# Tying the second MLP's weight decodings to their written place, and grouping its products into longer runs of matmuls

## The chip, the cores and the metric

One core of one Trainium2 chip runs the whole program. The engines that matter here are TensorE (PE; its weight loads stand apart as PEld), VectorE (DVE), ScalarE (ACT) and SyncE (SP), which here issues the DMA transfers. The metric is the device time of one execution in microseconds, the median of several runs.

## The reference

Everything is float32: 4 batches of 8 heads of 576 positions with 64 columns go through a linear attention, and the 2304 tokens of 512 columns that come out go through two MLPs with 2048 hidden columns.

```python
kv = einsum('bhsd,bhse->bhde', k, v)
out = einsum('bhsd,bhde->bhse', q, kv)
x = out / sqrt(mean(out * out, -1) + 1e-06) * g_norm      # as 2304 x 512
h = x @ w_in1;  x = (h * tanh(softplus(h))) @ w_out1      # first MLP
h = x @ w_in2                                             # second MLP
return (maximum(h, 0) + alpha * minimum(h, 0)) @ w_out2
```

## The kernel before

Every operand of a matmul is held as a high and a low part, and each product is three matmuls (`three`, L127 to L129): high by high, high by low, low by high. The weights come from DRAM as pairs of 32-bit words and are decoded on the chip: a scaling on ScalarE (`w_scale`, L387), three bit operations on VectorE (`w_bits`, L393, L394, L397), a cast to the high part on ScalarE (`w_high`, L432) and a subtraction for the low part on VectorE (`w_low`, L436). Each such operation covers 128 x 512 values.

**The first MLP** runs in 80 slots (NS = 80): five blocks of tokens by 16 blocks of hidden columns. In slot s TensorE does 12 matmuls of the first layer (tile `h`), ScalarE the activation of slot s-1 (`mish`, L502), ScalarE and VectorE split the result of slot s-2 into high and low (`g_split`, L495 and L496: tiles `gh`, `gl`), and TensorE does 12 matmuls of the second layer for slot s-4 (tile `acc`). The attention for later blocks is done between them.

**The second MLP** computes in three passes over 768 tokens, each of 8 units of hidden columns; the text numbers these units 0 to 23. A unit forms seven products of sums of blocks (`product`, "1", "6", "2", "7", "5", "4", "3"; six matmuls of 128 x 384 each, tile `pp`) and combines them to four blocks of the hidden layer, "11", "22", "21" and "12". The products share two banks of PSUM: 1, 2, 7 and 4 use one in turn, 6, 5 and 3 the other, so a product can start only when the sum that reads the last one in its bank has run (for product 2 the copy L805 on ScalarE, for 4 and 3 the sums L816 and L820 on VectorE, through the tiles `tx` and `ty`). Each block gets its PReLU (`prelu1`, L756 and L759), a cast to high on ScalarE (L761) and a subtraction for the low part on VectorE (L762, tiles `g` and `xb`), and enters the output by a chunk of nine matmuls of 128 x 512 (`chunk`, tile `acc`). A unit takes four quarters, one call of `unit` each: product 1, then the chunk of block 22 of the unit before; products 6 and 2, chunk 21 of the unit before; products 7 and 5, chunk 12 of the unit before; products 4 and 3, chunk 11 of the unit itself.

The second MLP's weights are prepared during the first MLP and the first pass. First-layer weights are decoded in eight pairs by `prep_unit` (five steps, with sums at L616 to L622 and splits at L572 and L573), written to DRAM (`put_unit`, L581, tile `wd`) and read back (`fetch`, `load_s`). Second-layer weights, 16 blocks j, are loaded by `load_out` (L375, tile `ws`) and decoded by `prep_out`. The table UNITS says in which slot or quarter (counted on from 80) a pair starts; t0 in the planning loop does it for the 16 blocks. The tokens' sums for the products are made from `xr` tiles, read from DRAM by L692 and added at L679, with high parts at L685 and low parts at L686.

TensorE's order is the written one from slot 20 on. On VectorE, ScalarE and SyncE a scheduler orders the instructions by its own timing, so an operation may stand well ahead of the place where it is written; each engine then runs its list strictly in order. Waiting for a transfer is part of an instruction, and whatever stands behind it on that engine waits too.

Of the kernel before, what the change touches and what calls it, by code (L numbers as in the profile page):

```python
# [13 lines left out]
ALU = mybir.AluOpType  # L14
# [19 lines left out]
EARLY = 4  # L34
WHEN = {1: (8, 3, 1, 2, 3, 6), 2: (4, 4, 1, 2, 3, 6), 3: (0, 5, 1, 2, 4, 5), 4: (0, 5, 1, 2, 4, 5)}
MANUAL = 20
IN_X = (4, 6)
UNITS = (36, 46, 51, 62, 65, 68, 70, 85)
BY32 = 2
FIRST = "p0 c0 p1 c1 p2 p3 c2 c3 w4 u0 w5 u1".split()  # L40
# [9 lines left out]
def attn_moe_moe2(  # L50
# [30 lines left out]
    nc = tc.nc  # L81
# [6 lines left out]
    NJ = DFF // P  # L88
# [4 lines left out]
    NS = NB * NJ  # L93
    NU = NJ // 2
    QW = 2 * P
    NPASS = NT // (2 * HT)
# [101 lines left out]
    def bank(tag, nm):  # L198
        if tag == "at":
            turn[0] += 1  # L200
            tag = f"at{turn[0] % 2}"
        pool = ps_h if tag == "h" else ps_a if tag[:2] == "at" else ps_acc
        return pool.tile([P, 512], F32, tag=tag, name=nm)
# [158 lines left out]
    def stage(nm, dt, cols):  # L362
        return st.tile([P, 2 * DM], dt, tag="ws", name=nm, bufs=3)[:, :cols]
# [164 lines left out]
    room1, xt, raw, pr, gg, tmp, acc1 = {}, {}, {}, {}, {}, {}, {}  # L528
# [56 lines left out]
    def place(i, nm):  # L585

        if (i, nm) not in places:
            if i not in IN_X:
                t = stage(nm, I32, 2 * DM) if nm in ("r0", "r1", "x") else st.tile([P, DM], F32, tag="wf", name="wf")
# [63 lines left out]
    def load_s(u, k):  # L653
        if u < NPASS * NU:
            room1["load"] = nc.sync.dma_start(out=f32(room1["ring"][k]), in_=wd["s", u % NU, k])
# [76 lines left out]
    def first_of(u, k):  # L732

        i = u % NU
        if k in "753":
            s = room1["ring"]["753".index(k)]
            h, l = s[:, :QW], s[:, QW:]
        else:
            h, l = w1[1, 2 * i + (k in "64")]
            h, l = ((t[:, QW:] if k in "24" else t[:, :QW]) for t in (h, l))  # L740
        return [(h[:, a * P : (a + 1) * P], l[:, a * P : (a + 1) * P]) for a in range(2)]

    def product(u, k):
        more = {"2": "1", "4": "7", "3": "5"}.get(k)
        if more:
            pr[u, k] = pr.pop((u, more))
        else:
            pr[u, k] = bank("h", "pp")[:, :HT]
        h, l = xt[TERMS[k]]
        for a, w in enumerate(first_of(u, k)):  # L750
            three(pr[u, k], w, (h[a], l[a]), not more and a == 0, a == 1, skip_group_check=bool(more))

    def prelu1(u, nm, src, out):
        j = 2 * (u % NU) + (nm[0] == "2")
        t = tmp["u"]
        nc.vector.tensor_scalar(  # L756
            out=t, in0=src, scalar1=0.0, scalar2=acol[:, j : j + 1], op0=ALU.min, op1=ALU.mult
        )
        nc.vector.scalar_tensor_tensor(out=out, in0=src, scalar=0.0, in1=t, op0=ALU.max, op1=ALU.add)  # L759
        h, l = gg[nm]  # L760
        nc.scalar.copy(out=h, in_=out)  # L761
        nc.vector.tensor_tensor(out=l, in0=out, in1=f32(h), op=ALU.subtract)  # L762

    def next_r():
        tmp["r"].reverse()
        return tmp["r"][0]
# [32 lines left out]
    def unit(u, step, before):  # L799

        x = tmp["x"]
        tt = nc.vector.tensor_tensor
        if step == 0:
            product(u, "1")
            nc.scalar.copy(out=x, in_=pr[u, "1"])  # L805
            before()
        elif step == 1:
            product(u, "6")
            tt(out=x, in0=pr.pop((u, "6")), in1=x, op=ALU.add)
            product(u, "2")  # L810
            prelu1(u, "11", pr.pop((u, "2")), next_r())
            before()
        elif step == 2:
            product(u, "7")
            r = next_r()
            tt(out=r, in0=pr[u, "7"], in1=x, op=ALU.add)  # L816
            load_s(u + 1, 0)
            product(u, "5")
            load_s(u + 1, 1)
            tt(out=r, in0=pr[u, "5"], in1=r, op=ALU.add)  # L820
            prelu1(u, "22", r, r)
            before()
        else:
            product(u, "4")
            r = next_r()
            tt(out=r, in0=pr.pop((u, "4")), in1=x, op=ALU.add)
            prelu1(u, "21", r, r)
            product(u, "3")
            load_s(u + 1, 2)
            tt(out=x, in0=pr.pop((u, "3")), in1=x, op=ALU.add)  # L830
            prelu1(u, "12", x, x)
            before()

    early, after, late, hook, mid, fin, last = ({} for _ in range(7))

    def add(d, s, f, *a):
        d.setdefault(s, []).append((f, a))

    def run(d, s):
        for f, a in d.pop(s, []):  # L840
            f(*a)

    new_kv = {1: 1, 2: 2, 3: 3}
    for i in range(1, NB):
        h0, step, dk, do, dm, db = WHEN[i]
        h0 += (i - 1) * 2 * NJ
        for p in range(NP):
            h = h0 + p * step
            pre, before = early, max((h - step + dk) // 2 + 1 if p else h // 2 - 2, EARLY)
            if i == 1 and p == 2:  # L850
                pre, before = after, before - 1
# [21 lines left out]
    for j in range(NJ):  # L873
        if j >= EARLY and (1, j) not in early_w:
            add(late, max(j - 3, EARLY), load_w, 0, 1, j)
            add(mid, j - 2, w_begin, 0, 1, j)
        if (2, j) not in early_w:
            add(early, max(j + 1, EARLY), load_w, 0, 2, j)
            add(last, j + 2, w_begin, 0, 2, j)
            add(mid, j + 3, w_end)  # L880
        add(early, max(NS - NJ + max(j, EARLY) + 1, UNITS[j // 2] + 6), fetch, 1, j)
        t0 = NS - 10 + 3 * j // 2 if j < 8 else NS + 2 * (j - 7)
        add(early, t0, load_out, j)
        add(fin, t0 + 2, prep_out, j, t0 + 2 < NS)
    for i, s in enumerate(UNITS):
        add(late, s, load_unit, i, 0)
        add(late, s + 1, load_unit, i, 1)
        for step in range(5):
            add(fin, s + (1, 2, 2, 3, 4)[step], prep_unit, i, step)
        for step in range(3):  # L890
            add(late, s + 3 + step, put_unit, i, step)
    add(early, NS - 5, rooms1)
    for n in range(2):
        add(early, NS - 5 + 2 * n, first_raw, n)
# [5 lines left out]
    for n in range(1, NPASS):  # L900
        t0 = NS + 4 * NU * n
# [4 lines left out]
    def front(s):  # L906
        if EARLY <= s <= NS:
            mish(s - 1)
# [19 lines left out]

    LATER = ("22", "21", "12", "11")

    def quarter(n):

        s = NS + n
        u, step = divmod(n, 4)
        run(early, s)
        run(late, s)

        def before():
            front(s)
            run(mid, s)  # L940
            back(s)
            if step == 3 or u:
                chunk(u if step == 3 else u - 1, LATER[step])

        if u < NPASS * NU:
            unit(u, step, before)
        else:
            before()
        run(fin, s)
        run(last, s)  # L950

# [31 lines left out]
    with tc.manual_schedule():  # L983
# [14 lines left out]
        for h in range(2):  # L998
            r = slice(h * D, (h + 1) * D)
# [5 lines left out]
        for p in range(NP):  # L1005
            for h in range(2):
                r = 32 * p + 16 * h
# [3 lines left out]
                    out=rows, in0=f32(rows), in1=ident[:, r + 1 : r + 2].to_broadcast([P, D]), op=ALU.add  # L1011
# [46 lines left out]
```

## Time and profile before

| what | value |
|---|---|
| median of 3 runs | 867.41 us (865.24 to 868.76) |
| the profiled execution's own time | 868.87 us |
| its span | 866.9 us |
| TensorE busy | 837.7 us (97%) |
| VectorE busy | 554.3 us (64%) |
| ScalarE busy | 317.6 us (37%) |

The profiled execution stands 1.5 us above the median. A row of a timeline gives an instruction's start and duration; matmuls overlap, so their spacing is read from one start to the next. What stands in brackets is the time that the engine was idle before it and what released it.

### The profile page before, as it was taken

What the parts mean: (1) busy time and instruction counts of PE and PEld (TensorE: products, weight loads), DVE (VectorE), ACT (ScalarE), POOL (GpSimd) and SP (SyncE); (2) the same over time, 40 slices, a digit from 0 to 9 for tenths busy, and PEclk for the clock granted to TensorE, in tenths of its full rate; (3) what the DMA queues carried; (4) which work ended last, traced back from release to release, by engine and by line L of the source; (5) the groups of instructions that cost most, each with busy time, mean ns of one, the idle gap of its engine ahead of it and who ended that gap; (6) DMA issues with size and microseconds to landing.
All of it is one profiled execution on the core that took longest, in us unless ns stands there. A gap on an engine that the chain in (4) does not pass through costs nothing.

```text
span 866.9 us, 11632 instructions
## 1 busy us (share of the span) xinstructions
PE 837.7 (97%) x4408; PEld 712.6 (82%) x4408; DVE 554.3 (64%) x1062; ACT 317.6 (37%) x619; POOL 1.3 (0%) x7
## 2 busy tenths in 40 slices
PE   7999899989999999999999989999999999999997
PEld 5678677888878887887888878898889888989996
DVE  5888966272576145655795797569665568655654
ACT  3776445434443254334564332114211124211111
POOL 0000000000000000000000000000000000000000
PEclk9999899999999999999999999999999999999999
DMA  9756464514631033027984741141321141411211
GB/s 242 223 153 190 143 159 98 123 24 92 222 134 25 1 132 135 1 97 277 349 333 158 244 156 50 37 134 49 110 63 47 52 132 37 134 49 37 61 49 73
DMA packets 84743, 104.58 MB, mean 121 GB/s; under 512 B 34768, under 2 KB 58832, under 8 KB 84688
## 3 DMA queue, kind: packets, MB, share of 16 engines
q1 hardware_dynamic: 84688, 103.84, 39.1%
q8 instruction: 35, 0.57, 0.3%
q14 instruction: 20, 0.16, 0.1%
HBM read 79.70 MB, written 24.12 MB: 120 GB/s over the span
## 4 chain that ended last, share of the span: by engine, by line
PE 73%; DVE 11%; DMA 9%; ACT 3%; SPq 2%; issue 2%; DVEq 0%; ACTq 0%
PE acc L127 12%; PE acc L129 12%; PE acc L128 12%; PE h L127 6%; PE pp L127 6%; PE pp L129 6%; PE pp L128 6%; PE h L128 6%; PE h L129 6%; DMA r<-in_moe_w_in_dram 2%; DMA v<-in_v_dram 2%; SPq L180 2%; DVE wf L394 1%; PE kvps L211 1%; DVE wf L397 1%
## 5 line engine op out<-in xcount | busy, mean ns | idle before, releaser
L127 PE MATMUL acc<-gh,w 128*128 128x512 f32 (+1 forms) x320 | 119.9, 375 | 0.9 <-ACT n L502 0.4
L129 PE MATMUL acc<-gh,w 128*128 128x512 f32 (+1 forms) x320 | 118.2, 369 | 0.0
L128 PE MATMUL acc<-gl,w 128*128 128x512 f32 (+1 forms) x320 | 118.2, 369 | 0.0
L127 PE MATMUL h<-x,w 128*128 128x512 f32 (+1 forms) x240 | 91.6, 381 | 4.6 <-ACT n L502 4.5
L129 PE MATMUL h<-x,w 128*128 128x512 f32 (+1 forms) x240 | 89.7, 374 | 0.8 <-DVE w L436 0.7
L128 PE MATMUL h<-x,w 128*128 128x512 f32 (+1 forms) x240 | 89.2, 372 | 0.0
L496 DVE TENSOR_TENSOR gl<-n,gh 128x512 fp32r<-128x512 f32 (+1 forms) x80 | 50.8, 634 | 57.2 <-ACT gh L495 56.8
L129 PE MATMUL acc<-w,g 128*128 128x512 f32 x216 | 85.6, 396 | 0.2
L761 ACT CAST g<-ty 128x384 fp32r<-128x384 f32 x48 | 24.8, 516 | 140.0 <-DVE ty L759 135.9
L495 ACT CAST gh<-n 128x512 fp32r<-128x512 f32 (+1 forms) x80 | 46.3, 579 | 66.1 <-PE acc L129 65.7
L127 PEld LDWEIGHTS acc<-gh,w 128*128 128x128 f32 x320 | 60.6, 189 | 12.0 <-ACT n L502 0.9
L129 PEld LDWEIGHTS acc<-gh,w 128*128 128x128 f32 x320 | 60.4, 189 | 10.6 <-DVE w L436 0.4
L128 PEld LDWEIGHTS acc<-gl,w 128*128 128x128 f32 x320 | 60.5, 189 | 9.7
L127 PEld LDWEIGHTS h<-x,w 128*128 128x128 f32 x240 | 45.6, 190 | 17.3 <-ACT n L502 7.0
L502 ACT ACTIVATE n<-h 128x512 f32<-128x512 f32 (+1 forms) x80 | 44.5, 556 | 34.7 <-DVE gl L496 33.8
L128 PE MATMUL acc<-w,xb 128*128 128x512 f32 x144 | 56.8, 395 | 0.0
L128 PE MATMUL acc<-w,g 128*128 128x512 f32 x144 | 56.8, 395 | 0.0
L127 PE MATMUL acc<-w,g 128*128 128x512 f32 x144 | 56.0, 389 | 0.0
L127 PE MATMUL acc<-w,xb 128*128 128x512 f32 x144 | 56.0, 389 | 0.0
L129 PEld LDWEIGHTS h<-x,w 128*128 128x128 f32 x240 | 45.7, 190 | 9.4 <-DVE w L436 1.6
L128 PEld LDWEIGHTS h<-x,w 128*128 128x128 f32 x240 | 45.7, 190 | 7.3
L129 PEld LDWEIGHTS acc<-w,g 128*128 128x128 f32 x216 | 40.5, 187 | 9.6 <-DVE g L762 1.1
(202 smaller groups left out, 1684.1 us busy)
## 6 DMA issues: line engine op xcount, KB each, us to landing
xb<-wd SPq DMA_DIRECT2D x72, 256.0 KB, 2.7
ws<-in_moe_w_out_dram SPq DMA_DIRECT2D x32, 512.0 KB, 4.3
ws<-in_moe_w_in_dram SPq DMA_DIRECT2D x16, 512.0 KB, 4.4
r<-in_moe_w_in_dram SPq DMA_DIRECT2D x12, 512.0 KB, 5.1
wd<-r SPq DMA_DIRECT2D x12, 512.0 KB, 3.5
w<-wd SPq DMA_DIRECT2D x12, 512.0 KB, 5.7
k<-in_k_dram SPq DMA_DIRECT2D x16, 288.0 KB, 3.8
v<-in_v_dram SPq DMA_DIRECT2D x16, 288.0 KB, 4.2
```

The source lines that it names most:

```text
L127: nc.tensor.matmul(ps, lh, rh, start=start, stop=False, **kw)
L128: nc.tensor.matmul(ps, lh, rl, start=False, stop=False, **kw)
L129: nc.tensor.matmul(ps, ll, rh, start=False, stop=stop, **kw)
L180: nc.sync.dma_start(out=t[r : r + 32, C * p0 : C * (p0 + n)].rearrange("p (b d) -> p b d", d=32), in_=q[b, h, s : s + C * n, d : d + 32].r ...
L211: nc.tensor.matmul(ps[hs, hs], kt[:, h, j, :], vt[:, h, j, :], start=(j == 0), stop=(j == KVJ - 1))
L394: nc.vector.scalar_tensor_tensor(out=si, in0=high, scalar=-0x80000000, in1=si, op0=ALU.bitwise_and, op1=ALU.bitwise_or)
L397: nc.vector.scalar_tensor_tensor(out=si, in0=high, scalar=3, in1=si, op0=ALU.logical_shift_left, op1=ALU.bitwise_or)
L495: nc.scalar.copy(out=gh, in_=g)
L496: nc.vector.tensor_tensor(out=gl, in0=g, in1=f32(gh), op=ALU.subtract)
L502: nc.scalar.activation(out=g, in_=hps.pop(kk)[:, :T], func=AF.Mish)
L761: nc.scalar.copy(out=h, in_=out)
```

## The change

Three things change. First, `behind` wraps each `prep_unit` and `prep_out`: their instructions are ordered after the VectorE and ScalarE instructions that are written just before them, so they cannot stand earlier in these engines' lists. Second, the places are written anew: second-layer blocks 0 to 5 are decoded in slots 72 to 79 and loaded two slots earlier; blocks 6 to 15 are decoded in quarters 0, 1, 4, 5, 16, 17, 20, 21, 24 and 25 of the second MLP and loaded four quarters earlier; the last pair of first-layer weights (place 85) has its steps spread over quarters 8 to 16 with later puts and a later fetch. Third, twelve units (9 to 14 and 17 to 22) are done by `long_unit`: products 1, 6, 2 together, then two chunks of the unit before, then products 7, 5, 4, 3 together, then chunk 12 of the unit before and chunk 11 of the unit itself.

```diff
--- before.py
+++ after.py
@@ -35,6 +35,8 @@
 WHEN = {1: (8, 3, 1, 2, 3, 6), 2: (4, 4, 1, 2, 3, 6), 3: (0, 5, 1, 2, 4, 5), 4: (0, 5, 1, 2, 4, 5)}
 MANUAL = 20
 IN_X = (4, 6)
+SOON = 6
+OUTS = (0, 1, 4, 5, 16, 17, 20, 21, 24, 25)
 UNITS = (36, 46, 51, 62, 65, 68, 70, 85)
 BY32 = 2
 FIRST = "p0 c0 p1 c1 p2 p3 c2 c3 w4 u0 w5 u1".split()
@@ -830,6 +832,42 @@
             tt(out=x, in0=pr.pop((u, "3")), in1=x, op=ALU.add)
             prelu1(u, "12", x, x)
             before()
+
+    def long_unit(u, step):
+
+        x = tmp["x"]
+        tt = nc.vector.tensor_tensor
+        if step == 0:
+            product(u, "1")
+            nc.scalar.copy(out=x, in_=pr[u, "1"])
+            product(u, "6")
+            tt(out=x, in0=pr.pop((u, "6")), in1=x, op=ALU.add)
+            product(u, "2")
+            prelu1(u, "11", pr.pop((u, "2")), next_r())
+        elif step == 2:
+            product(u, "7")
+            r = next_r()
+            tt(out=r, in0=pr[u, "7"], in1=x, op=ALU.add)
+            load_s(u + 1, 0)
+            product(u, "5")
+            load_s(u + 1, 1)
+            tt(out=r, in0=pr[u, "5"], in1=r, op=ALU.add)
+            product(u, "4")
+            r2 = next_r()
+            tt(out=r2, in0=pr.pop((u, "4")), in1=x, op=ALU.add)
+            product(u, "3")
+            load_s(u + 1, 2)
+            tt(out=x, in0=pr.pop((u, "3")), in1=x, op=ALU.add)
+            prelu1(u, "22", r, r)
+            prelu1(u, "21", r2, r2)
+
+    def behind(f, *a):
+
+        with ExitStack() as stack:
+            for e in (mybir.EngineType.DVE, mybir.EngineType.Activation):
+                prev = next(i for i in reversed(nc.cur_bb.bb.instructions) if i.engine == e)
+                stack.enter_context(tc.issue_after(prev))
+            f(*a)
 
     early, after, late, hook, mid, fin, last = ({} for _ in range(7))
 
@@ -878,17 +916,18 @@
             add(early, max(j + 1, EARLY), load_w, 0, 2, j)
             add(last, j + 2, w_begin, 0, 2, j)
             add(mid, j + 3, w_end)
-        add(early, max(NS - NJ + max(j, EARLY) + 1, UNITS[j // 2] + 6), fetch, 1, j)
-        t0 = NS - 10 + 3 * j // 2 if j < 8 else NS + 2 * (j - 7)
-        add(early, t0, load_out, j)
-        add(fin, t0 + 2, prep_out, j, t0 + 2 < NS)
+        add(early, max(NS - NJ + max(j, EARLY) + 1, UNITS[j // 2] + (6 if j // 2 < NU - 1 else 14)), fetch, 1, j)
+        t0 = NS - 8 + 3 * j // 2 if j < SOON else NS + OUTS[j - SOON]
+        add(early, t0 - (2 if j < SOON else 4), load_out, j)
+        add(fin, t0, behind, prep_out, j, j < SOON)
     for i, s in enumerate(UNITS):
+        steps, puts = ((1, 2, 2, 3, 4), (3, 4, 5)) if i < NU - 1 else ((3, 4, 7, 8, 11), (8, 9, 12))
         add(late, s, load_unit, i, 0)
         add(late, s + 1, load_unit, i, 1)
         for step in range(5):
-            add(fin, s + (1, 2, 2, 3, 4)[step], prep_unit, i, step)
+            add(fin, s + steps[step], behind, prep_unit, i, step)
         for step in range(3):
-            add(late, s + 3 + step, put_unit, i, step)
+            add(late, s + puts[step], put_unit, i, step)
     add(early, NS - 5, rooms1)
     for n in range(2):
         add(early, NS - 5 + 2 * n, first_raw, n)
@@ -928,6 +967,9 @@
 
     LATER = ("22", "21", "12", "11")
 
+    def long(u):
+        return NU < u < NPASS * NU and 0 < u % NU < NU - 1
+
     def quarter(n):
 
         s = NS + n
@@ -935,17 +977,26 @@
         run(early, s)
         run(late, s)
 
-        def before():
+        def before(step):
             front(s)
             run(mid, s)
             back(s)
             if step == 3 or u:
                 chunk(u if step == 3 else u - 1, LATER[step])
 
-        if u < NPASS * NU:
-            unit(u, step, before)
+        if long(u):
+            long_unit(u, step)
+            if step == 1:
+                before(0)
+                before(1)
+            elif step == 3:
+                before(2)
+                prelu1(u, "12", tmp["x"], tmp["x"])
+                before(3)
+        elif u < NPASS * NU:
+            unit(u, step, lambda: before(step))
         else:
-            before()
+            before(step)
         run(fin, s)
         run(last, s)
```

From line 37 on, a line of the changed kernel has a number that is higher by 2 (L816 becomes L818) as far as the new functions.

In VectorE's list at the end of unit 1, behind the sum L826, this stands before (`wf` with `ws` is a second-layer block, `r0` and `x_4658` a first-layer pair, `ty`, `tx`, `tu` and `g1` belong to unit 1):

```order
L573 TENSOR_TENSOR x_4658<-wf_4583,x_4658 128x256
L393 TENSOR_SCALAR wf_4651<-ws_4539 128x512
L756 TENSOR_SCALAR tu_4302<-ty_4300,acol_93 128x384
L830 TENSOR_TENSOR tx_4299<-pp_4552,tx_4299 128x384
L762 TENSOR_TENSOR g1_4304<-ty_4300,g1_4303 128x384
L393 TENSOR_SCALAR wf_4737<-ws_4629 128x512
L394 SCALAR_TENSOR_TENSOR wf_4651<-ws_4539,wf_4651 128x512
L759 SCALAR_TENSOR_TENSOR ty_4300<-ty_4300,tu_4302 128x384
L394 SCALAR_TENSOR_TENSOR wf_4737<-ws_4629,wf_4737 128x512
L397 SCALAR_TENSOR_TENSOR wf_4651<-ws_4539,wf_4651 128x512
L756 TENSOR_SCALAR tu_4302<-tx_4299,acol_93 128x384
L762 TENSOR_TENSOR g1_4306<-ty_4300,g1_4305 128x384
```

and now, with the same sum (L828) as its first row:

```order
L828 TENSOR_TENSOR ty_4302<-pp_4549,tx_4301 128x384
L758 TENSOR_SCALAR tu_4304<-ty_4302,acol_93 128x384
L832 TENSOR_TENSOR tx_4301<-pp_4558,tx_4301 128x384
L761 SCALAR_TENSOR_TENSOR ty_4302<-ty_4302,tu_4304 128x384
L758 TENSOR_SCALAR tu_4304<-tx_4301,acol_93 128x384
L761 SCALAR_TENSOR_TENSOR tx_4301<-tx_4301,tu_4304 128x384
L764 TENSOR_TENSOR g1_4308<-ty_4302,g1_4307 128x384
L764 TENSOR_TENSOR g1_4303<-tx_4301,xb_4300 128x384
L395 TENSOR_SCALAR wf_4630<-r0_4510 128x512
L396 SCALAR_TENSOR_TENSOR wf_4630<-r0_4510,wf_4630 128x512
L399 SCALAR_TENSOR_TENSOR wf_4630<-r0_4510,wf_4630 128x512
L811 TENSOR_TENSOR tx_4301<-pp_4634,tx_4301 128x384
```

The second-layer blocks have left this place: unit 1's own eight operations follow one another, a first-layer decoding stands behind them, and then comes unit 2's first sum.

In TensorE's list, from unit 9's product 7 on (the first of six or nine matmuls of each product or chunk; `pp` is a product, `acc` a chunk, the row above it the end of chunk 21 of unit 8), before:

```order
L127 MATMUL acc_5517<-w21_3969,g1_4305 128x512
...
L127 MATMUL pp_5576<-xt_4051,xb_4298 128x384
...
L127 MATMUL pp_5585<-xa_4040,xb_4298 128x384
...
L127 MATMUL acc_5537<-w20_3911,xb_4298 128x512
...
L127 MATMUL pp_5576<-xa_4040,w1first_3732 128x384
...
L127 MATMUL pp_5585<-xa_4040,xb_4298 128x384
...
L127 MATMUL acc_5517<-w22_4080,xb_4298 128x512
...
L127 MATMUL pp_5639<-xt_4041,w14_3737 128x384
```

and now, on into unit 10:

```order
L129 MATMUL acc_5517<-w21_3969,g1_4307 128x512
...
L129 MATMUL pp_5576<-xt_4051,xb_4300 128x384
...
L129 MATMUL pp_5585<-xa_4040,xb_4300 128x384
...
L129 MATMUL pp_5576<-xa_4040,w1first_3732 128x384
...
L129 MATMUL pp_5585<-xa_4040,xb_4300 128x384
...
L129 MATMUL acc_5555<-w20_3911,xb_4300 128x512
...
L129 MATMUL acc_5517<-w22_4080,xb_4300 128x512
...
L129 MATMUL pp_5639<-xt_4041,w14_3737 128x384
...
L129 MATMUL pp_5647<-xt_4045,w15_3787 128x384
...
L129 MATMUL pp_5639<-xt_4049,w14_3737 128x384
...
L129 MATMUL acc_5555<-w23_4125,g1_4305 128x512
```

The chunk between products 5 and 4 (its weights are `w20`) has moved behind product 3, next to the chunk with `w22`, and in unit 10 products 1, 6 and 2 stand in one run ahead of two chunks.

In SyncE's list at the end of the first MLP (`ws` are loads of second-layer blocks, `xr` reads the tokens of the first pass, `w112` and its like fetch first-layer weights), before, where the rows end ahead of `load_s`:

```order
L375 DMA ws_4255<-in_moe2_w_out_dram 128x1024
L651 DMA w111_4101<-wd_3958 128x1024
L692 DMA xr_4166<-x2d_1466 128x768
L375 DMA ws_4296<-in_moe2_w_out_dram 128x1024
L651 DMA w112_4162<-wd_3960 128x1024
L375 DMA ws_4381<-in_moe2_w_out_dram 128x1024
L651 DMA w113_4199<-wd_4071 128x1024
L375 DMA ws_4480<-in_moe2_w_out_dram 128x1024
L375 DMA ws_4539<-in_moe2_w_out_dram 128x1024
```

and now:

```order
L694 DMA xr_4168<-x2d_1466 128x768
L653 DMA w112_4166<-wd_3960 128x1024
L583 DMA wd_4071<-xw_3564 128x1024
L377 DMA ws_4298<-in_moe2_w_out_dram 128x1024
L377 DMA ws_4349<-in_moe2_w_out_dram 128x1024
L653 DMA w113_4203<-wd_4071 128x1024
L377 DMA ws_4729<-in_moe2_w_out_dram 128x1024
L694 DMA xr_4170<-x2d_1466 128x768
L657 DMA xb_4300<-wd_2490 128x512
```

Behind the fourth `xr` load (`xr_4166`) stood the four loads of second-layer blocks 7 to 10. Now the loads of blocks 8, 9 and 10 stand ahead of it (`xr_4170`), that of block 10 (`ws_4729`) directly, and behind it comes `load_s`.

## Rows read from the trace of the kernel before

**Rows 1.** the page's first part: busy us of each engine, share of the span, instructions.

```profile
PE 837.7 (97%) x4408; PEld 712.6 (82%) x4408; DVE 554.3 (64%) x1062; ACT 317.6 (37%) x619; POOL 1.3 (0%) x7
```

**Rows 2.** busy us by stretch: length, PE, PEld, DVE, ACT, POOL, PEclk, DMA, GB/s.

```profile
500.00:520.00 20.00, 16.09 (x79) 13.74 (x78) 20.00 (x42) 6.14 (x12) 0.00 (x0) 1.00 0.40 140
540.00:560.00 20.00, 20.00 (x102) 18.04 (x101) 9.98 (x20) 3.52 (x7) 0.00 (x0) 1.00 0.15 40
```

**Rows 3.** the waits: engine, line, what was waited for: us, times, longest us.

```profile
DVE wf L393 <- DMA r<-in_moe_w_in_dram: 22.5, 8, 5.0
```

**Rows 4.** TensorE's groups of instructions, 220 to 400 us; idle time before them last.

```profile
L127 PE MATMUL h<-x,w 128*128 128x512 f32 x92 | 36.5, 397 | 0.4 <-ACT n L502 0.3
...
L127 PE MATMUL h<-x,w1first 128*128 128x512 f32 x32 | 12.6, 393 | 1.0 <-ACT n L502 1.0
```

**Rows 5.** TensorE's timeline around three waits: start us, us, instruction [idle before <-releaser].

```profile
394.99 0.39 PE L129 MATMUL acc<-gh,w 128*128 128x512 f32 x1
396.38 0.50 PE L127 MATMUL h<-x,w1first 128*128 128x512 f32 x1 [1.01 <-ACT n L502]
...
507.82 0.34 PE L129 MATMUL pp<-xt,w 128*128 128x384 f32 x1
511.45 0.44 PE L127 MATMUL pp<-xt,w 128*128 128x384 f32 x1 [3.29 <-ACT tx L805]
...
518.68 0.40 PE L129 MATMUL acc<-w,g 128*128 128x512 f32 x1
519.70 0.45 PE L127 MATMUL pp<-xa,w 128*128 128x384 f32 x1 [0.62 <-DVE ty L816]
```

**Rows 6.** ScalarE's timeline at 395 us, same columns.

```profile
395.18 0.67 ACT L387 ACTIVATE xw<-xw 128x512 f32<-128x512 f32 x1 [4.58 <-DMA xw<-in_moe_w_in_dram]
395.75 0.58 ACT L502 ACTIVATE n<-h 128x512 f32<-128x512 f32 x1
```

**Rows 7.** VectorE's timeline ahead of 511.45 us.

```profile
508.73 1.29 DVE L436 TENSOR_TENSOR w<-wf,w 128x512 fp32r<-128x512 f32 x2
...
510.27 0.56 DVE L762 TENSOR_TENSOR g<-tx,xb 128x384 fp32r<-128x384 f32 x1
```

**Rows 8.** ScalarE's timeline ahead of 511.45 us.

```profile
510.91 0.48 ACT L805 COPY tx<-pp 128x384 f32<-128x384 f32 x1 [1.50 <-DVE g L762]
```

**Rows 9.** SyncE's queue at the end of slot 78 of the first MLP.

```profile
462.37 0.33 SPq L375 DMA_DIRECT2D ws<-in_moe_w_out_dram  x1
```

**Rows 10.** transfers of the tile xr, 425 to 475 us.

```profile
DMA to landing us min/median/max: 4.2/6.3/7.6
```

**Rows 11.** VectorE's timeline at 468 us.

```profile
468.47 0.69 DVE L496 TENSOR_TENSOR gl<-n,gh 128x512 fp32r<-128x512 f32 x1 [1.22 <-ACT gh L495]
```

**Rows 12.** TensorE's timeline in product 6 of unit 0.

```profile
472.15 0.34 PE L128 MATMUL pp<-xt,w1first 128*128 128x384 f32 x1
```

**Rows 13.** TensorE's timeline in unit 10 and behind the last unit.

```profile
635.93 0.39 PE L127 MATMUL acc<-w,g 128*128 128x512 f32 x1
...
638.01 0.33 PE L127 MATMUL pp<-xt,w 128*128 128x384 f32 x1
...
642.19 0.33 PE L127 MATMUL pp<-xt,xb 128*128 128x384 f32 x1
...
643.26 0.33 PE L127 MATMUL pp<-xa,xb 128*128 128x384 f32 x1
...
644.30 0.39 PE L127 MATMUL acc<-w,xb 128*128 128x512 f32 x1
...
855.93 0.39 PE L127 MATMUL acc<-w,g 128*128 128x512 f32 x1
...
857.97 0.39 PE L127 MATMUL acc<-w,g 128*128 128x512 f32 x1
```

**Rows 14.** VectorE's timeline, sums that free product banks in unit 10.

```profile
643.46 0.56 DVE L816 TENSOR_TENSOR ty<-pp,tx 128x384 f32<-128x384 f32 x1 [0.80 <-PE pp L129]
644.50 0.56 DVE L820 TENSOR_TENSOR ty<-pp,ty 128x384 f32<-128x384 f32 x1 [0.48 <-PE pp L129]
```


## Prediction

> **What bounds the kernel now.** I read the page's first part, then the windows, then every place after 220 us where TensorE's starts lie further apart than usual. TensorE is busy for 97% of the span [rows 1], so a change that leaves its matmuls as they are can win only in the rest and in the spacing of the matmuls. Both MLPs' matmuls are the same in number and shape after the change. In 540 to 560 us the picture is the ordinary one of the second MLP: TensorE 20.00 of 20 us, VectorE 9.98. In 500 to 520 us it is turned round: VectorE 20.00 of 20, TensorE 16.09 [rows 2]. In that one stretch VectorE is the bound, and the difference of 10.0 us on VectorE is decoding.
>
> The chain at 511.45 us, in unit 2: the last matmul of product 6 starts at 507.82, that of product 2 at 511.45, and TensorE waited 3.29 us for the copy into `tx` [rows 5]. The copy on ScalarE began at 510.91, after 1.50 us of waiting for a low part on VectorE [rows 8]. That low part (L762) began only at 510.27; directly before it two decodings' L436 took 1.29 us [rows 7], and more decoding stands between the unit's operations ahead of that, as the order of before at the end of unit 1 shows. So the products waited because operations of a unit stood behind decodings of weights that unit did not need yet. The wait at 519.70, for the sum L816, has the same neighbours [rows 5].
>
> The earlier stall at 396.38 has another form: an instruction that waits for a transfer holds its engine. ScalarE's scaling at 395.18 had been idle for 4.58 us until a load of weights landed, the activation behind it could start only at 395.75 [rows 6], and TensorE's next slot waited for that activation: 1.39 us between starts [rows 5]. VectorE has eight such waits of its own for first-layer weights, 22.5 us in all and up to 5.0 us [rows 3]; most cost TensorE nothing.
>
> **What the tying takes away.** In the first MLP from 220 to 400 us TensorE's idle time before first-layer matmuls is 0.4 and 1.0 us [rows 4]. The 1.0 is the stall at 396.38, which by starts is 1.39 less the ordinary 0.23 (one 512-column step: 2.08 over 9), so 1.16 [rows 5, 13]: 1.6 us with the other. In the second MLP, 511.45 less 507.82 is 3.63, less the ordinary 0.18 (1.07 over 6) is 3.45; 519.70 less 518.68 is 1.02, less 0.23 is 0.79 [rows 5, 13]. Each of these two also refills slowly: about 0.1 us each, my estimate from the first matmul's 0.44 and 0.45 us against 0.33 for one of its kind that follows without a wait [rows 5, 13]. Together 1.6 + 3.45 + 0.79 + 0.2 = 6.0 us.
>
> Do they all go? In the new order the decodings stand behind the operations that are written before them. A second-layer block now has four quarters, a whole unit, between load and decoding (two slots in the first MLP), so it should find its data. A unit's own work on VectorE is 9.98 of 20 us [rows 2], or 7.8 of the unit's 15.7 (42 starts of 0.175 and 36 of 0.23), which leaves 7.9 us for decodings; no unit now gets more than two second-layer blocks or two steps of the last pair, and a block's decoding is two or three us by its L436 (0.65 each) and three operations of the same size [rows 7]. So the decodings fit in each unit, though not with much room, and I take the whole 6.0. The bounds: nothing beyond 6.0, since only these waits are counted; at the other end the first-layer pairs have only one slot between load and decoding, and a tied decoding that waits can hold VectorE or ScalarE as at 395.18. One such wait cost up to 1.16 us, and four pairs lie close together in slots 62 to 70 with the last blocks behind them: up to 4.6 us back. I take 0, because most such waits already cost TensorE nothing [rows 3, 4].
>
> **What the long runs take away.** The first nine 512-column matmuls after a product take 2.08 us (635.93 to 638.01), a second nine in the same run 2.04 (855.93 to 857.97). The first six of 384 columns after a chunk take 1.07 (642.19 to 643.26), the next six 1.04 (643.26 to 644.30) [rows 13]. A change of shape so costs 0.04 + 0.03 = 0.07 us for the way there and back. A unit of before has four such pairs, a long one two; 12 units by 2 by 0.07 is 1.7 us. Nothing hides this and nothing can hide behind it, since TensorE is the bound there [rows 2].
>
> The Trainium skill bears on this term (TensorE: Matmul & The Clock Gate, Back-to-back issue gap): there the spacing of warm matmuls depends on their columns alone, so grouping would be worth nothing. Its formula for one matmul gives an estimate of 216 ns at 512 columns, where the rows have 227 to 231, and they differ by position in the run, so here the measurement decides.
>
> **What the change costs.** (a) The fourth `xr` load now stands in SyncE's queue behind the load of block 10, which waits until the second-layer matmuls of slot 78 have read the old weights. In before that same load of block 10 is issued at 462.37 [rows 9]. The `xr` load is then issued at about 462.7 and lands 4.2 to 7.6 us later [rows 10], between 466.9 and 470.3, with little traffic by then, so nearer 467. VectorE's next operation in its list is the `gl` at 468.47 [rows 11], done at 469.16; behind it, by the new order, are two sums, one L436, and four low parts up to the last one of product 6's operand (0.47 to 0.6 us each when they follow closely, as the 0.56 and 0.65 of L762 and L436 show [rows 7]): 7 by 0.47 to 0.6 is 3.3 to 4.2 us, less one operation that may slip in ahead, so 472.5 to 473.5. TensorE reads that operand at 472.15 [rows 12]. So 0.4 to 1.4 us are lost; a landing at 470.3 would make it 2.5, and a landing early enough with less on VectorE none. I take 1.0.
>
> (b) In a long unit products 7, 5, 4, 3 follow one another in two banks. Product 4 needs the sum behind product 7, which ends at 643.46 + 0.56 = 644.02; it would start where 644.30 stands. Product 3 needs the sum that ends at 645.06 and would start at 644.30 + 1.04 = 645.34 [rows 13, 14]. Each has 0.28 us to spare, less what the signal and the weight load ahead of the matmul take; no row of before has this sequence. Nearest are these two sums, which started 0.2 us after the matmul before them (product 5's start 643.26, the sum 643.46). From both sides: no loss, or for 24 handovers 0.1 us and its refill of 0.1, 4.8 us. I take 0.3, near the lower end, because VectorE has no decoding left in these units and is idle half the time [rows 2].
>
> (c) Everything else that is moved (puts, the last fetch, `load_s`) has a whole unit or more to spare, and I cost it at nothing; what covers it is the 0.15 DMA share of a steady unit [rows 2].
>
> **The sum.** Against the profiled execution: 868.9 - 6.0 - 1.7 + 1.0 + 0.3 = 862.5 us. That execution was 1.5 us above the median of the runs, so the median to expect is 861.0.
>
> **Rivals.**
> 1. The tied decodings wait themselves. Their place in the lists is now fixed, so a late transfer or a full VectorE in units 0 to 5 holds everything behind it. For it: eight such waits are in the trace already [rows 3], and first-layer pairs have one slot only. Against it: loads were moved earlier together with the places, and VectorE has room. It takes back 2 to 6 us: 863 to 867.
> 2. The order of runs is worth nothing (the rule above as a mechanism): 861.0 + 1.7 = 862.7. Against it stand 2.08 and 2.04 us for the same nine matmuls [rows 13].
> 3. The bank handover is a little late. Each of the 24 waits 0.1 to 0.2 us: 2.4 to 4.8 more, 863.1 to 865.5.
> 4. Slower: the handover is really late. Products 4 and 3 of the twelve long units have no chunk between them and the sums they wait for; in before a chunk of 2.08 us stood there. If a late sum or its signal makes each wait 0.6 us, 24 of them are 14 us, 875. From 0.45 us each (24 by 0.45 is 10.8) the kernel is slower beyond what can be told. For it: the same two-bank handover stopped TensorE at 511.45 and 519.70 [rows 5]. Against it: there VectorE was full, and 0.28 us to spare would have to become 0.45 us late.
>
> **How the numbers follow.** About 4.3 us (0.5%) is what a measurement of this kernel tells from no change: faster is below 863.1, slower above 871.7. The forecast holds 0.57 (859.0 to 862.9, from no cost of (a) and (b) to the upper end of (a)), rival 2 0.08, rival 1 0.18, rival 3 0.10, rival 4 0.07. The forecast, rival 2 in part and a little of rival 1 lie below 863.1: 0.67. Rivals 1 and 3 with the rest: 0.26. Slower: 0.07. The range of 8 in 10 runs from 858.5, no cost and a quicker run by 2.5, to 866.5, near the upper end of rival 1.
>
> **What would show it.** In the new profile: VectorE below 20 of 20 us in the stretch around 510, no gap above 0.5 us before products 2 and 4 of unit 2 (the 3.45 and 0.79); no ScalarE scaling that holds an activation near 395 (1.16); 2.08 + 2.04 us for eighteen chunk matmuls in a long unit, and some 0.14 us less for the whole unit (1.7); a gap of 0.4 to 1.4 us in product 6 of unit 0 (a); products 4 and 3 of long units starting 0.18 us after the last matmul before them (b). It is wrong if the two MLPs show new waits on transfers ahead of tied decodings, or if a long unit takes longer than a steady one of before.

## The result and the profile after

The changed kernel takes 857.26 us (median of 6 runs, 856.55 to 859.91) against 867.47 us (6 runs, 865.24 to 870.51): a ratio of 0.9889, interval 0.9863 to 0.9915, or 7.4 to 11.9 us less. It is faster, by more than the forecast of 6.4 us, and 857.26 lies below the range of 858.5 to 866.5.

The two programs start their matmuls in the same order up to the first long unit, so the starts can be laid side by side by their position in the order. The table gives the time from one such matmul to the next; the stretches are named by where they lie in the trace of before. The last stretch ends seven matmuls (1.6 us) ahead of the last one; the row "all" goes on to the last matmul. Before and after were each traced twice (e5 and e6 are the second traces).

| stretch (us in before) | before | before, e5 | after | after, e6 | forecast of the change |
|---|---|---|---|---|---|
| start to 225.9 | 225.93 | 223.28 | 224.76 | 223.64 | 0 |
| 225.9 to 465.8 (first MLP) | 239.87 | 239.53 | 237.13 | 237.13 | -1.6 |
| 465.8 to 490.8 (units 0, 1) | 24.96 | 24.96 | 26.01 | 26.01 | +1.0 |
| 490.8 to 523.3 (units 1 to 3) | 32.54 | 32.97 | 28.04 | 28.04 | -4.4 |
| 523.3 to 603.6 | 80.29 | 80.29 | 80.38 | 80.39 | 0 |
| 603.6 to the end | 256.65 | 256.54 | 254.72 | 254.69 | -1.7 + 0.3 |
| all behind 225.9, to the last matmul | 635.90 | 635.87 | 627.87 | 627.85 | -6.4 |

Behind the first 225 us (the head, below) the change is worth 8.0 us, and both pairs of traces repeat that within 0.05. The head differs by 2.7 us between two traces of one and the same program; what the medians show beyond 8.0 us is within their interval and need not be the change. The median of before itself was 866.01 us in a later series of 20 runs, 867.18 in one of 8 and 868.47 in one of 7.

The page's first part, as in [rows 1]:

```profile
PE 836.0 (97%) x4408; PEld 714.5 (83%) x4408; DVE 550.7 (64%) x1062; ACT 314.1 (37%) x619; POOL 1.3 (0%) x7
```

The windows, as in [rows 2]; then the one row of the waits that answers to [rows 3]:

```profile
500.00:520.00 20.00, 20.00 (x100) 17.86 (x99) 15.65 (x32) 5.71 (x11) 0.00 (x0) 1.00 0.19 53
540.00:560.00 20.00, 20.00 (x101) 18.04 (x101) 16.95 (x34) 6.30 (x13) 0.00 (x0) 1.00 0.37 114
```

```profile
DVE wf L395 <- DMA r<-in_moe_w_in_dram: 13.4, 5, 5.0
```

VectorE is no longer full in the stretch where it was the bound, and TensorE is busy all the time there. In 540 to 560 us VectorE has the decodings now: 16.95 of 20 us, and TensorE does not notice. First-layer decodings still wait for transfers, 5 times instead of 8.

TensorE's timeline where the waits of [rows 5] stood: the first slot's matmul of 396.38, product 2 and product 4 of unit 2.

```profile
392.75 0.39 PE L131 MATMUL acc<-gh,w 128*128 128x512 f32 x1
392.98 0.39 PE L129 MATMUL h<-x,w1first 128*128 128x512 f32 x1
...
504.95 0.34 PE L131 MATMUL pp<-xt,w 128*128 128x384 f32 x1
505.13 0.33 PE L129 MATMUL pp<-xt,w 128*128 128x384 f32 x1
...
512.21 0.39 PE L131 MATMUL acc<-w,g 128*128 128x512 f32 x1
512.44 0.33 PE L129 MATMUL pp<-xa,w 128*128 128x384 f32 x1
```

Starts are 0.23, 0.18 and 0.23 us apart: the three waits are gone. The new one is in product 6 of unit 0, as in [rows 12]; below it are SyncE's two issues ([rows 9]), the landing of that load ([rows 10]) and VectorE's list ([rows 11]).

```profile
468.05 0.33 PE L129 MATMUL pp<-xt,w1first 128*128 128x384 f32 x1
469.18 0.44 PE L130 MATMUL pp<-xt,w1first 128*128 128x384 f32 x1 [0.80 <-DVE xt L688]
```

```profile
458.45 0.33 SPq L377 DMA_DIRECT2D ws<-in_moe_w_out_dram  x1
459.29 0.33 SPq L694 DMA_DIRECT2D xr<-x2d  x1
```

```profile
DMA to landing us min/median/max: 4.0/4.0/4.0
```

```profile
464.55 0.69 DVE L498 TENSOR_TENSOR gl<-n,gh 128x512 fp32r<-128x512 f32 x1 [1.11 <-ACT gh L497]
465.16 0.55 DVE L681 TENSOR_TENSOR xr<-xr 128x384 f32<-128x384 f32 x1
...
468.57 0.56 DVE L688 TENSOR_TENSOR xt<-xr,xt 128x384 fp32r<-128x384 f32 x1
```

1.13 us instead of 0.18. The load of block 10 goes out at 458.45, `xr` right behind it at 459.29, and it lands after 4.0 us, at 463.3. So it was in time; VectorE reached the first sum only at 465.16, behind `gl`, and the last low part of the seven operations that follow ended at 469.13.

A long unit on TensorE (eighteen matmuls of two chunks, then products 7, 5, 4), as in [rows 13], and the two sums that free the banks, as in [rows 14]:

```profile
614.99 0.39 PE L129 MATMUL acc<-w,g 128*128 128x512 f32 x1
...
617.07 0.39 PE L129 MATMUL acc<-w,g 128*128 128x512 f32 x1
...
619.11 0.33 PE L129 MATMUL pp<-xt,xb 128*128 128x384 f32 x1
...
620.18 0.33 PE L129 MATMUL pp<-xa,xb 128*128 128x384 f32 x1
...
621.22 0.33 PE L129 MATMUL pp<-xa,w1first 128*128 128x384 f32 x1
```

```profile
620.38 0.56 DVE L850 TENSOR_TENSOR ty<-pp,tx 128x384 f32<-128x384 f32 x1 [2.84 <-PE pp L131]
621.42 0.56 DVE L854 TENSOR_TENSOR ty<-pp,ty 128x384 f32<-128x384 f32 x1 [0.48 <-PE pp L131]
```

The chunks take 2.08 and 2.04 us, product 4 starts at 621.22 right after product 5 and no handover waits in any of the twelve units.

### The profile page after: what moved, and what is told of

The parts are those of the page before. It is cut to its first block, busy times and chain, and to the rows that moved or that the text cites. A ratio compares the mean times of both kernels' runs of the same rounds, so it can differ in the third digit from the quotient of the medians.

```text
span 857.7 us, 11635 instructions
## 1 busy us (share of the span) xinstructions
PE 836.0 (97%) x4408; PEld 714.5 (83%) x4408; DVE 550.7 (64%) x1062; ACT 314.1 (37%) x619; POOL 1.3 (0%) x7
## 4 chain that ended last, share of the span: by engine, by line
PE 79%; DVE 9%; DMA 6%; ACT 3%; SPq 2%; issue 1%; DVEq 0%; ACTq 0%
PE acc L129 13%; PE acc L131 13%; PE acc L130 13%; PE h L129 6%; PE pp L129 6%; PE pp L131 6%; PE pp L130 6%; PE h L131 6%; PE h L130 6%; DMA v<-in_v_dram 3%; DMA ws<-in_moe_w_in_dram 2%; SPq L182 2%; PE kvps L213 1%; DVE wf L396 1%; DVE wf L399 1%
## 5 line engine op out<-in xcount | busy, mean ns | idle before, releaser
L129 PEld LDWEIGHTS h<-x,w 128*128 128x128 f32 x240 | 46.4, 193 | 16.4 <-ACT n L504 6.1
L131 PEld LDWEIGHTS h<-x,w 128*128 128x128 f32 x240 | 46.6, 194 | 9.4 <-DVE w L438 1.6
L130 PEld LDWEIGHTS h<-x,w 128*128 128x128 f32 x240 | 46.4, 193 | 7.6
```

The source lines that it names most:

```text
L129: nc.tensor.matmul(ps, lh, rh, start=start, stop=False, **kw)
L130: nc.tensor.matmul(ps, lh, rl, start=False, stop=False, **kw)
L131: nc.tensor.matmul(ps, ll, rh, start=False, stop=stop, **kw)
```

## The experiments

Times of stretches below are the same as in the table. Lines of after and of all runs made from it are 2 or more higher than before's.

**e1, long runs taken out.**

```diff
 def long(u):
-    return NU < u < NPASS * NU and 0 < u % NU < NU - 1
+    return False
```

> The changed kernel with all units done in eight short runs, as before; decodings as changed. Theory (each change of matmul shape costs 0.03 to 0.04 us, so the long runs give 24 pairs x 0.07): 1.6 to 1.9 us longer than the changed kernel, 858.9 to 859.2 beside its 857.3, all of it from unit 9 on, spread evenly, 0.13 to 0.15 per unit. Rival (the spacing of matmuls does not depend on the order of runs, and the 1.8 us that the changed kernel won behind 540 us is something else): same stretch as in the changed kernel, 857.3.

Measured: 859.41 us (857.65 to 860.59). All stretches up to 523 us are those of the changed kernel to 0.01, and the next takes 0.14 more; from 603.6 us on it takes 257.43 instead of 254.72, 2.71 more. Of that 1.15 is one wait with its refill before product 5 of unit 14, which the changed kernel has not (VectorE, waiting for the next pass's tokens from DRAM, holds up the PReLU that reads product 2; in before the same place costs 0.26 in the first trace and 0.12 in the second). 1.5 us are spread over the twelve units, 15.71 us instead of 15.57 in ten of them and 0.09 in units 9 and 17. This wait also tells of the banks: product 5 follows product 2 in its bank, and 7 follows 6, the other way round than the section on the kernel before has it. For 4 behind 7 and 3 behind 5 that changes nothing. The rival is out; the size is 0.13 us a unit, where the expectation had 0.13 to 0.15.

**e2, the tie taken out.**

```diff
 def behind(f, *a):
-        for e in (mybir.EngineType.DVE, mybir.EngineType.Activation):
+        for e in ():
```

> The changed kernel with the new places and the long runs, but without the tie: the scheduler may again order decodings ahead of their place. Theory (the tie took the stalls away): the waits before products 2 and 4 of unit 2 come back, 3.4 and 0.8 us with their refills, and one or more of the three before first-layer matmuls of slots (0.46, 0.27, 1.17); about 4 to 6.5 us longer than the changed kernel, 861 to 864. Rival (the new places and earlier loads did it, the tie only writes it down): no wait above 0.5 us there, 857 to 858.

Measured: 865.99 us (862.07 to 866.62), no different from before (ratio 0.9988, 0.9969 to 1.0006). The first MLP takes 240.12 us again, units 1 to 3 even 34.26. From 603.6 us on it keeps what the long runs give (254.76 instead of 256.65). Without the tie the places win nothing; the rival is out. The wait before product 2 of unit 2 is back at 3.54 us between starts, and behind it TensorE runs at its lower clock. Its timeline, and the window around it:

```profile
508.22 0.69 PE L129 MATMUL pp<-xt,w 128*128 128x384 f32 x1 [3.20 <-ACT tx L807]
508.71 0.52 PE L130 MATMUL pp<-xt,w 128*128 128x384 f32 x1
509.03 0.52 PE L131 MATMUL pp<-xt,w 128*128 128x384 f32 x1
...
510.31 0.63 PE L129 MATMUL acc<-w,g 128*128 128x512 f32 x1
510.73 0.63 PE L130 MATMUL acc<-w,g 128*128 128x512 f32 x1
```

```profile
495.00:515.00 20.00, 16.80 (x70) 14.52 (x69) 20.00 (x44) 6.64 (x13) 0.00 (x0) 0.83 0.41 152
```

Six matmuls of 384 columns follow 0.32 us apart instead of 0.17, then nine of 512 columns 0.43 apart instead of 0.23: 2.8 us on top of the wait, at a granted clock of 0.83 over these 20 us, where it dropped to its 1.2 GHz level.

**e3, only second-layer blocks tied.**

```diff
-            add(fin, s + steps[step], behind, prep_unit, i, step)
+            add(fin, s + steps[step], prep_unit, i, step)
```

> The changed kernel with only the second-layer blocks tied to their place; the first-layer pairs are free again. Theory (the waits in unit 2 came from second-layer blocks, those in the first MLP from first-layer pairs): no wait in unit 2; the three in the first MLP are back in some form, 1.5 to 2.5 us with refills, so 859 to 860. Rival (both kinds share VectorE, and either alone is enough to bring back the unit 2 waits): 861 to 863.

Measured: 863.68 us (861.76 to 868.81). My theory fell in its first half: the first MLP is back at 239.67 as it said, but the wait in unit 2 stays too (32.38 in units 1 to 3):

```profile
504.94 0.34 PE L131 MATMUL pp<-xt,w 128*128 128x384 f32 x1
507.80 0.69 PE L129 MATMUL pp<-xt,w 128*128 128x384 f32 x1 [2.51 <-ACT tx L807]
```

In its list VectorE does the last first-layer pair (tiles `r`, `x`, `wf`), now free, between unit 1's operations. So it is not the second-layer blocks as such that stop unit 2: a first-layer pair that moves into the same place does it too.

**e9, only first-layer pairs tied** (run after e3, to see whether the pairs' tie alone does it).

```diff
-        add(fin, t0, behind, prep_out, j, j < SOON)
+        add(fin, t0, prep_out, j, j < SOON)
```

> The changed kernel with only the first-layer pairs tied; the second-layer blocks may be ordered freely again (the opposite of the run that tied these alone). Theory, as amended by that run (the wait in unit 2 needs one more decoding than VectorE has room for in units 1 and 2, whichever kind it is; here the tied last pair keeps out of unit 1): the three waits of the first MLP stay away, 237.1 us from 225 to 465 us as in the changed kernel; no wait in unit 2, 28.0 to 28.5 us there; behind the first 225 us the same 627.9 us as the changed kernel within 1. Rival (free second-layer blocks clog unit 2 as in the kernel before): 2.5 to 4.5 us longer in unit 2.

Measured: 861.63 us (859.23 to 862.13). The first MLP (237.13) and unit 2 (28.04) are as in the changed kernel, as expected; but 523.3 to 603.6 takes 83.28 instead of 80.38. The wait has moved to unit 4: product 2 starts 1.97 us and product 5 1.07 us behind the matmul ahead of it. So the expected 627.9 us behind the head became 630.82. TensorE there, then VectorE:

```profile
536.08 0.34 PE L131 MATMUL pp<-xt,w 128*128 128x384 f32 x1
538.05 0.44 PE L129 MATMUL pp<-xt,w 128*128 128x384 f32 x1 [1.63 <-ACT tx L807]
```

```profile
535.68 1.28 DVE L399 SCALAR_TENSOR_TENSOR wf<-ws,wf 128x512 int32<-128x512 int32 x2
536.88 0.55 DVE L764 TENSOR_TENSOR g<-tx,xb 128x384 fp32r<-128x384 f32 x1
```

Two free decodings' operations again stand right before the low part that the copy waits for. So both ties are needed, each for its own place.

**e10, the kernel before with its first seven pairs tied to their old places** (the function `behind` is put into it as well).

```diff
-            add(fin, s + (1, 2, 2, 3, 4)[step], prep_unit, i, step)
+            add(fin, s + (1, 2, 2, 3, 4)[step], *((behind, prep_unit) if i < 7 else (prep_unit,)), i, step)
```

> The kernel before with its first seven first-layer pairs tied to their old places, nothing else. Theory (the waits of the first MLP come from these pairs alone): 237.1 instead of 239.5 to 239.9 us from 225 to 465 us, and the stretch of unit 2 stays at 32.5 to 33.0, so 2.5 to 2.8 us less behind the head than the kernel before. Rival (the tie at the old places makes decodings wait for transfers in new spots): 239 or more in that stretch.

Measured in a single run: 866.24 us; 237.13 in the first MLP, 32.95 in units 1 to 3. The tie of the pairs alone takes the whole 2.4 to 2.7 us from the first MLP. It also brings the gap in unit 0 (26.02 from 465.8 to 490.8), which the second-layer blocks' new places are therefore not needed for: in this kernel's order block 10's load stands ahead of the `xr` load too. But behind the head only 0.3 us of the expected 2.5 to 2.8 is left (635.58 instead of 635.90): the gap in unit 0 takes 1.06, a wait before product 5 of unit 6 (1.26 us from start to start) with its refill 1.19, and units 1 to 3 are 0.4 longer at a lower clock. No run ties both kinds of decoding to their old places, so whether unit 2 needs the second-layer blocks' new places beside the tie is not shown.

**e4, the `xr` load ahead of block 10's.**

```diff
 def load_out(j):
+        with ExitStack() as stack:
+            if j >= 10:
+                stack.enter_context(tc.issue_after(room1["xr"]))
+            load_out_at(j)
+
+    def load_out_at(j):
...
             nc.sync.dma_start(out=t, in_=x2d[0][:, c, : 2 * HT])
+            room1["xr"] = next(i for i in reversed(nc.cur_bb.bb.instructions) if i.engine == mybir.EngineType.SP)
```

For block 10 and those behind it `room1["xr"]` is the fourth `xr` load.

> The changed kernel with the fourth token load of the second MLP ahead of the load of second-layer block 10 in SyncE's queue, nothing else. Theory (term (a) of the prediction: that load waits behind block 10's, which waits for slot 78): the 1.13 us gap in product 6 of unit 0 shrinks to the usual 0.18, so 0.95 to 1.1 us shorter than the changed kernel, about 856.2. Rival (the gap is VectorE's own list, the low parts queued behind gl, and the load is not the last to come): the gap stays at 0.8 us or more.

Measured: 857.98 us (856.1 to 859.03). The gap is gone:

```profile
466.70 0.35 PE L129 MATMUL pp<-xt,w1first 128*128 128x384 f32 x1
466.89 0.34 PE L130 MATMUL pp<-xt,w1first 128*128 128x384 f32 x1
```

The stretch from 465.8 takes 25.14 instead of 26.01. With the load earlier VectorE's list also has the first sums ahead of `gl`, so this run does not part the queue from the list:

```profile
461.99 0.55 DVE L687 TENSOR_TENSOR xr<-xr 128x384 f32<-128x384 f32 x1
...
463.86 0.68 DVE L498 TENSOR_TENSOR gl<-n,gh 128x512 fp32r<-128x512 f32 x1
```

Four smaller waits elsewhere (0.1 to 0.2 us each) gave most of it back, and behind 225 us the whole is 627.63 against 627.87: the lowest of all, but not a difference that the medians can show.

**e7, one more operation ahead of the sum that frees product 7's bank.**

```diff
         r = next_r()
+        nc.vector.tensor_copy(out=tmp["u"], in_=pr[u, "7"])
         tt(out=r, in0=pr[u, "7"], in1=x, op=ALU.add)
```

> The changed kernel with one more VectorE copy of 128 x 384 out of product 7's bank ahead of the sum that frees this bank, in each of the twelve long units; it computes nothing that is used. Theory (product 4 has 0.28 us or less to spare behind that sum, and nothing else waits): the sum ends 0.4 to 0.6 us later, so product 4 starts 0.15 to 0.35 late with a refill of 0.1 in each unit, 12 x 0.25 to 0.45 = 3 to 5.4 us longer than the changed kernel. Rival (the handover has more to spare than the trace of before says): under 1 us in all. What decides rival 4 of the prediction: if one extra operation costs over 0.9 us per unit, this handover could have made the change slower.

Measured in a single run: 861.81 us; 259.01 instead of 254.72 from 603.6 us on, 4.3 us. VectorE, then TensorE, in unit 9:

```profile
618.37 0.56 DVE L850 COPY tu<-pp 128x384 f32<-128x384 f32 x1 [2.84 <-PE pp L131]
618.85 0.55 DVE L851 TENSOR_TENSOR ty<-pp,tx 128x384 f32<-128x384 f32 x1
```

```profile
619.04 0.34 PE L131 MATMUL pp<-xa,xb 128*128 128x384 f32 x1
619.45 0.44 PE L129 MATMUL pp<-xa,w1first 128*128 128x384 f32 x1
```

The sum starts 0.48 later and product 4 stands 0.41 us behind the last matmul instead of 0.17, so 0.24 late: 0.24 us were to spare. With the refill of 0.1 each of the twelve long units loses 0.34. The mechanism of the prediction's rivals 3 and 4, a late handover, is real and near: one operation more in this place costs more (4.3 us) than the long runs give in spacing (1.5).

**e8, long units in the first pass too,** with e4's load.

```diff
-        return NU < u < NPASS * NU and 0 < u % NU < NU - 1
+        return u < NPASS * NU and 0 < u % NU < NU - 1
```

> The changed kernel with the token load ahead of block 10's load, and long units in the first pass too (units 1 to 6, where decodings share VectorE). Theory (0.134 us per long unit wherever VectorE is in time): 6 x 0.134 = 0.8 us less in the first pass than with the token load alone, 855.5 to 856.5, no new wait. Rival (in units 1 to 4 the decodings stand between the sums that free the banks, and products 4 and 3 come late): gaps of 0.3 to 1.5 us in some of these units, 856.5 to 859.

Measured: 859.12 us (858.05 to 860.74). From 465.8 to 603.6 it takes 135.58 us, e4 133.68: 1.9 longer, not 0.8 shorter. In units 1 to 6 product 2 waits three times for its copy (0.2 to 0.8 us late) and product 3 four times (0.1 to 0.4 late). The longest is in unit 5:

```profile
548.11 0.34 PE L131 MATMUL pp<-xt,w 128*128 128x384 f32 x1
549.05 0.44 PE L129 MATMUL pp<-xt,w 128*128 128x384 f32 x1 [0.60 <-ACT tx L849]
```

The rival held for product 3; the copy ahead of product 2 it had not named. Where decodings share VectorE, the reserve of a long unit is not enough.

**e11, the kernel before with the long units** (the functions `long_unit`, `long` and the new `quarter` put into it).

> The kernel before with the twelve long units and its old decodings. Theory (the long runs are worth 0.134 us a unit by themselves and meet no wait): the stretch from 603 us on 1.6 to 1.9 us shorter than before's 256.6, all stretches ahead of it as before (239.5 to 239.9, 24.96, 32.5 to 33). Rival (without the new places the decodings make the sums of long units late): 256 or more.

Measured in a single run: 868.12 us, of it 226.13 in the head. From 603.6 us on 254.77 instead of 256.5 to 256.65; units 1 to 3 as before, 32.48. The first pass has one wait before a product 5 like that in e1, 0.85 us from start to start, which takes 0.77 of it back; behind the head 634.92 us are left of 635.90. From 603.6 us on the long units are so worth 1.8 to 1.9 us by themselves, 0.13 us in each of ten units again, with the small wait that before has in unit 14.

**e5 and e6, before and after once more.**

> The kernel before, once more, for a second trace. Theory (the first 225 us vary between executions of one program, and the rest repeats): the stretch up to 225 us differs from the first trace's 224.5 us by up to 4 us, from there to the end of the span it is within 0.5 us of the first trace, unless the clock is halved behind the 3.45 us wait of unit 2, as in the run without the tie and in the one with half of it: then 1.5 to 3 us longer there. Rival (the head is the same in all executions of this kernel, and the change shortened it by some unseen way): head again 224 to 225.

> The changed kernel once more, for a second trace. Theory: head anywhere in 220 to 225 us, behind it 634.3 us up to the last matmul's row as in the first trace, within 0.5. Rival (head shortened by the change): head within 0.5 of 223.3.

Measured: 866.19 and 858.36 us. The heads are 223.28 and 223.64, where the other traces have 225.93 and 224.76; over all thirteen traces the head lies between 221.8 and 226.1 us, whichever kernel. Behind it both repeat to 0.03. In e5 the clock fell behind the wait in unit 2, unlike in the first trace:

```profile
500.00:520.00 20.00, 16.62 (x77) 14.79 (x76) 20.00 (x41) 5.74 (x11) 0.00 (x0) 0.91 0.30 104
```

The granted clock is 0.91 over this stretch; it cost 1.3 us, of which 0.9 came back, since product 4's sum was then in time.

## Why the prediction was wrong

Its mechanisms were right, and the sum of them too small. Of the 3.8 us between the forecast's 6.4 and the medians' 10.2, 1.6 us lie behind the head: 1.1 in the first MLP, 0.3 in (b) and 0.2 in the stretch of the long runs. The other 2.2 us are not found there. By the prediction's own steps:

- **"1.6 us with the other", the first MLP: the step that failed.** It measured 2.74 us against the first trace of before and 2.40 against the second. I took the idle time of a view that groups instructions, 0.4 us for two waits, where the starts of the matmuls have 0.46 and 0.27 beyond the usual:

```profile
237.97 0.39 PE L129 MATMUL acc<-gh,w 128*128 128x512 f32 x1
238.66 0.50 PE L127 MATMUL h<-x,w 128*128 128x512 f32 x1 [0.30 <-ACT n L502]
...
331.81 0.39 PE L129 MATMUL acc<-gh,w 128*128 128x512 f32 x1
332.31 0.50 PE L127 MATMUL h<-x,w 128*128 128x512 f32 x1
332.65 0.40 PE L128 MATMUL h<-x,w 128*128 128x512 f32 x1
```

0.69 and 0.50 us from the matmul ahead, where 0.23 is usual. And I gave none of these waits a refill, which both here and later is 0.11 us in the matmul after a wait (332.65 less 332.31 is 0.34 instead of 0.23); two slots after the wait at 396.38 have it as well. The three waits (0.46, 0.27 and 1.17), five such refills (0.55), a late start at 402.05 (0.09) and 0.2 spread over the rest make the 2.74; in the second trace the same waits are 0.29, 0.21 and 0.81, with one of 0.22 in a later slot. With this step the bound "nothing beyond 6.0" fell as well: 2.74 + 4.50 is 7.24.
- **3.45 + 0.79 + 0.2 in unit 2:** right, 4.50 for 4.44. What they rest on, decodings that stand ahead of unit 2's operations, is shown by e2; that the second-layer blocks alone are meant was too narrow (e3, e9).
- **1.7 us of the long runs:** right in the main. The stretch is 1.93 us shorter, of which the spacing of the matmuls is 1.5 (e1, e11: 0.13 a unit for the 0.14 that was worked out); the other 0.4 are small waits that got shorter, 0.26 of it before product 5 of unit 14, which the prediction did not have. So 1.93 comes near 1.7 partly by luck. Rival 2 does not hold here: the same matmuls in other groups take 1.5 us less. The prediction had taken it from the formula that the Trainium skill gives for the isolated gap (TensorE: Matmul & The Clock Gate, Back-to-back issue gap), which has the columns alone in it; for a stream that section has the weight load set the spacing as well.
- **1.0 us for (a):** right, 1.05, and by the path that was worked out: the load lands ahead of `gl`, and the seven operations behind `gl` set the time. That the load stands behind block 10's does not come from the new places alone, since tying the pairs does it too (e10); and e4 changes VectorE's list with the queue.
- **0.3 us for (b):** nothing was lost; the reserve was 0.24 us (e7) where 0.28 was read.
- **Rival 1** (tied decodings wait): they do, 13.4 us on VectorE, and behind 225 us no gap of TensorE falls to them.
- **The range** was too high at its lower end by its own words: "no cost and a quicker run by 2.5" is 861.0 - 1.3 - 2.5 = 857.2, not 858.5, and the forecast's 859.0 "from no cost" should be 859.7. The head varies by some 4 us over the traces, and medians of six runs moved by 10.2 us where the change is worth 8.0. That the other 2.2 us are head and clock is likely by the traces, but not shown: most of the timed runs have no trace.

## What to carry to other kernels

Where an engine runs its list in order, read what stands between two operations of the bound chain before you read how busy the engine is: work that is needed much later, moved ahead by a scheduler, stops the chain as surely as a missing operand, and if only half of that work is tied down the other half moves into the gap. Price a wait by the starts of the instructions around it and add the slow ones behind it. When matmuls of two shapes alternate, group them only where the sums between them have some tenths of a microsecond to spare.

## What the runs showed of the hardware

A change from 384 to 512 columns costs 0.04 us in all in the spacing of the nine matmuls that follow (2.08 instead of 2.04), one from 512 to 384 columns 0.03 us in the six that follow (1.07 instead of 1.04). A wait costs 0.11 us more in the first matmul behind it. The wait before product 2 of unit 2 was followed in some traces by TensorE's lower clock level, 1.2 GHz, for 7 to 15 matmuls, which cost 1.3 to 2.8 us: in e2, e3, e5 and e10, where TensorE had been idle for 3.20, 2.51, 3.38 and 3.08 us (granted clock 0.83 over 20 us in e2, 0.91 in the others). In others it was not: in the first trace of before and in e11, after 3.29 and 3.23 us.
